# Attention in chunks of 64 tokens as four 64x64 tiles of TensorE, heads exchanged in odd chunks

## The chip, the cores and the metric

One core of a Trainium2 chip runs the whole kernel. The metric is device microseconds of one execution, from the host's launch to the end on the core. Times are medians of several runs; the profile is one execution taken by the hardware profiler.

## The reference

Linear attention with a decay per head, over 4 sequences of 768 tokens, 8 heads of 64, and behind it a SwiGLU layer on the 3072 rows of 512:

```python
block = 64
for b in range(nb):
    intra = einsum('bhic,bhjc->bhij', qb, kb) * Dmask          # lam ** (i - j), i >= j
    intra = einsum('bhij,bhjd->bhid', intra, vb)
    inter = einsum('bhid,bhde->bhie', qb * lam_pow, kv_state)  # lam ** (i + 1)
    out[:, :, sl] = intra + inter
    kv_state = lam_block * kv_state + einsum('bhsd,bhse->bhde', kb * rev_pow, vb)
x = out as rows of (token, head * 64)
xn = x / sqrt(mean(x * x) + 1e-6) * rms_g
g = xn @ w_gate; val = xn @ w_val                              # 512 x 1536
y = (g * sigmoid(g) * val) @ w_out                             # 1536 x 512
```

All is float32. The result of the attention does not depend on the size of the chunks, so a kernel may choose its own.

## The kernel before

Tokens go in six groups of 512 (`G`, four chunks of 128, `GC`), heads in four pairs (`NP`). Two heads of 64 fill the 128 partitions. So there are 24 pairs of work, `Pair(m, p)`, group m and pair of heads p. The attention works in float32, and each float32 matmul of the program is two instructions on TensorE.

A pair has four kinds of matmul, each for four chunks and two heads. `scores` multiplies keys and queries of a chunk, 64 rows by 128 columns of the array for each head, into two banks of PSUM (`pa`, banks ps0 and ps1). `state_sums` sums keys and values over the 128 tokens of a chunk, 128 rows by 64 columns (`pst`). `mix_chunks` multiplies the decayed scores with the values, 128 rows by 64 columns (`po`), and `mix_states` adds the state before the chunk times the query, 64 rows by 64 columns, into the same `po`. VectorE multiplies the scores with the decay table (`decay_a`, one operation of 128x512 for each head) and carries the state from chunk to chunk (`states`, one operation of 128x64 for each chunk). ScalarE scales the keys (`decay_k`), copies the output into the rows (`keep_output`) and squares it (`keep_squares`); GpSimd scales the queries (`decay_q`). `powers` makes the decay tables by scans on VectorE.

The layer behind runs in units (group m, 128 hidden columns f). Units of groups 0 and 1 use plain products (`gate`, `val`, L761) with weights split into f16 halves, and beside them the weights are converted, scaled and summed on VectorE, ScalarE and GpSimd. From group 2 on (after some 260 us of the span) each unit is a two-by-two scheme of seven smaller products (L948, 128x256). The output products are L780 to L782. Units of that scheme take turns between the banks ps0, ps1 and the banks pg, pv; a pair of the next group is laid beside them: its scores in a unit that leaves ps0 and ps1 free, the rest in the next one, which leaves pg and pv free. `pst` and `po` lie in pg and pv (po0 and po1 for a few early pairs). The small column sums for the weights (L445, L321) use ps1.

The order of all engines comes from a planner in the kernel's own code (`Plan`): each step has an engine, a cost, a due time, what it reads and writes and which buffers it opens. `SHIFTS` moves the due times of single steps by their number. The planner charges TensorE a small price where the kind of matmul changes (`TURN`).

## Time and profile before

| | |
|---|---|
| median of 3 runs | 653.84 us (653.78 to 654.0) |
| span of the profiled execution | 652.3 us; of its whole time the page gives no more |
| TensorE busy (matmuls) | 642.5 us, 98%, 5016 matmuls |
| VectorE busy | 433.9 us, 67%, 836 instructions |
| ScalarE busy | 334.8 us, 51%, 676 instructions |
| GpSimd busy | 149.4 us, 23%, 133 instructions |

A matmul's time runs from its start to its modelled end, and several are in flight at once, so the busy time of one group of matmuls is more than the time it takes up: a row of "x16" has the time from the first start to the last end. How far apart matmuls start has to be read from the starts. "Idle before" is the time in which an engine had nothing, and behind the arrow stands what ended it.

### The profile page before, as it was taken

The page shows a single profiled execution, that of the slowest core. Times are in us where ns is not written, and L with a number is a line of the kernel's source. Part 1 is how long each engine was busy: PE and PEld are TensorE (multiplying, and loading weights), DVE is VectorE, ACT ScalarE, POOL GpSimd, SP SyncE. Part 2 cuts the span into 40 slices and gives each one's busy share as a digit, 9 for nine tenths or more (in the row PEclk, how much of TensorE's full clock was granted, in tenths as well). Part 3 has the DMA queues.
Part 4 walks back from the last instruction along what each step waited for, and adds up shares of the span by engine and source line. Part 5 has one row for each costly group of instructions (what it writes and reads, how often), then busy time and mean ns, then how long its engine had stood idle before and what let it go on. Part 6 is the DMA issues. An engine that isn't in the chain of part 4 may idle for free.

```text
span 652.3 us, 12342 instructions
## 1 busy us (share of the span) xinstructions
PE 642.5 (98%) x5016; PEld 442.0 (68%) x5016; DVE 433.9 (67%) x836; ACT 334.8 (51%) x676; POOL 149.4 (23%) x133
## 2 busy tenths in 40 slices
PE   7999999999999999999999999999999999999997
PEld 6846564755656645777777777777777777777774
DVE  6798897968997659656589634587543488544334
ACT  2876876756774444444545533335444334533332
POOL 2213040003477654354703011002010101100000
PEclk9999999999999999999999999999999999999999
DMA  8956653411002400101300311100220000000001
GB/s 328 327 211 221 238 191 133 169 58 65 1 24 91 146 2 1 65 4 63 130 2 2 130 65 65 66 1 1 97 99 1 2 2 1 33 33 1 2 1 65
DMA packets 14314, 51.13 MB, mean 78 GB/s; under 512 B 1713, under 2 KB 1969, under 8 KB 12849
## 3 DMA queue, kind: packets, MB, share of 16 engines
q1 hardware_dynamic: 13968, 50.21, 21.5%
q8 instruction: 39, 0.64, 0.4%
q10 hardware_dynamic: 288, 0.14, 0.1%
q14 instruction: 19, 0.15, 0.1%
HBM read 44.05 MB, written 6.29 MB: 77 GB/s over the span
## 4 chain that ended last, share of the span: by engine, by line
PE 95%; DVE 3%; DMA 1%; issue 0%; POOL 0%; ACT 0%; DVEq 0%; ACTq 0%
PE pa L948 20%; PE pb L948 15%; PE acc L780 10%; PE acc L782 10%; PE acc L781 10%; PE pg L761 9%; PE pv L761 9%; PE pa L507 4%; PE po L572 3%; PE po L583 3%; PE pst L540 2%; PE pss L628 1%; DMA cs<-in_consts_dram 1%; DVE xn L714 0%; DVE pw L159 0%
## 5 line engine op out<-in xcount | busy, mean ns | idle before, releaser
L996 ACT COPY tx<-pa 128x256 f32<-128x256 f32 x144 | 53.6, 372 | 136.6 <-PE pa L948 134.9
L782 PE MATMUL acc<-wo,hh 128*128 128x512 f16 (+1 forms) x288 | 110.2, 383 | 0.0
L781 PE MATMUL acc<-wo,hh 128*128 128x512 f16 (+1 forms) x288 | 110.1, 382 | 0.0
L1000 DVE TENSOR_TENSOR tx<-pb,tx 128x256 f32<-128x256 f32 x96 | 40.8, 425 | 65.3 <-PE pb L948 59.9
L780 PE MATMUL acc<-wo,hh 128*128 128x512 f16 x216 | 81.8, 379 | 0.0
L1004 DVE TENSOR_TENSOR sg<-pb,tx 128x256 f32<-128x256 f32 x48 | 20.4, 425 | 78.5 <-ACT tx L996 76.1
L948 PEld LDWEIGHTS <-wo 128*128 128x128 f16 x576 | 54.9, 98 | 23.2 <-issue 1.7
L761 PE MATMUL pg<-x,wg 128*128 128x512 f16 x288 | 67.7, 379 | 1.3 <-DVE wg L467 0.7
L761 PE MATMUL pv<-x,wv 128*128 128x512 f16 x288 | 67.5, 379 | 0.0
L948 PEld LDWEIGHTS <-wg 128*128 128x128 f16 x576 | 56.3, 98 | 16.2 <-issue 0.3
L1041 ACT CAST hh<-sg 128x512 f16<-128x512 f32 (+2 forms) x73 | 44.7, 612 | 35.6 <-DVE sg L1016 15.4
L948 PEld LDWEIGHTS <-wv 128*128 128x128 f16 x576 | 56.3, 98 | 8.3 <-issue 0.2
L531 POOL TENSOR_TENSOR qkv<-qkv,pw 128x512 f32<-128x512 f32 x24 | 32.2, 1342 | 77.3 <-PE pa L507 71.1
L761 PEld LDWEIGHTS <-wg 128*128 128x128 f16 x288 | 26.8, 98 | 33.8 <-issue 2.4
L761 PEld LDWEIGHTS <-wv 128*128 128x128 f16 x288 | 27.1, 98 | 32.9 <-issue 1.2
L1052 DVE TENSOR_TENSOR hh<-sg,hh 128x512 f16<-128x512 f32 x53 | 39.2, 739 | 7.8 <-ACT hh L1041 3.5
L1016 DVE SCALAR_TENSOR_TENSOR sg<-tx,cv,sg 128x512 f32<-128x512 f32 (+1 forms) x49 | 39.3, 803 | 5.6 <-ACT sg L1008 0.7
L948 PE MATMUL pa<-tx,wo 128*128 128x256 f16 x288 | 39.4, 273 | 0.0
L948 PE MATMUL pb<-tx,wo 128*128 128x256 f16 x288 | 39.3, 273 | 0.0
L948 PE MATMUL pa<-x,wv 128*128 128x256 f16 x288 | 39.3, 273 | 0.0
L948 PE MATMUL pa<-x,wg 128*128 128x256 f16 x288 | 39.3, 273 | 0.0
L948 PE MATMUL pb<-x,wv 128*128 128x256 f16 x288 | 39.3, 273 | 0.0
(186 smaller groups left out, 1152.1 us busy)
## 6 DMA issues: line engine op xcount, KB each, us to landing
qkv<-in_qkv_dram SPq DMA_DIRECT2D x48, 512.0 KB, 4.8
raw_gv<-in_weights_dram SPq DMA_DIRECT2D x11, 1024.0 KB, 6.3
raw_o<-in_weights_dram SPq DMA_DIRECT2D x12, 512.0 KB, 4.1
out_dram<-o SPq DMA_DIRECT2D x23, 256.0 KB, 2.1
partial<-in_weights_dram SPq DMA_DIRECT2D x2, 512.0 KB, 11.1
out_dram<-o ACTq DMA_DIRECT2D x1, 128.0 KB, 2.4
out_dram<-o SPq DMA_DIRECT2D x1, 128.0 KB, 2.4
cs<-in_consts_dram ACTq DMA_DIRECT2D x1, 8.0 KB, 4.7
```

Of the source, the lines that this page charges most:

```text
L507: nc.tensor.matmul(self.pa[j][:, c, :], self.kT[r, c, :], self.qT[r, c, :], start=True, stop=True,)
L531: eng.tensor_mul(self.qT, self.qT, pw[:, p : p + 1, :].broadcast_to([P, GC, P]))
L761: nc.tensor.matmul(ps, w[:, kk, :], x[:, kk, :], start=i == kk == 0, stop=i == 2 and kk == NK - 1,)
L780: nc.tensor.matmul(acc[:, cols], hl[:, ts_], oh, start=first, stop=False, skip_group_check=True)
L781: nc.tensor.matmul(acc[:, cols], hh[:, ts_], ol, start=False, stop=False, skip_group_check=True)
L782: nc.tensor.matmul(acc[:, cols], hh[:, ts_], oh, start=False, stop=last, skip_group_check=True)
L948: nc.tensor.matmul(ps, w(ow, k), x(ox, k), start=first and i == k == 0, stop=i == 2 and k == 1, skip_group_check=True,)
L996: nc.scalar.copy(self.kept[:, i], self.pa)
L1000: nc.vector.tensor_add(self.val[:, half], self.pb, self.kept[:, i])
L1016: nc.vector.scalar_tensor_tensor(sg, self.val[:, half], cv[:, self.f : self.f + 1], sg, ALU.mult, ALU.mult)
L1041: nc.scalar.copy(self.hh[:, half], self.sg[:, half])
L1052: nc.vector.tensor_sub(self.hl, self.sg, hh)
```

## The change

Chunks of 64 tokens in place of 128. A chunk c of 128 tokens stays the unit of the loops and of the layout; it is now an even and an odd half (o = 0, 1). In odd halves the host has exchanged the two heads of a pair in q, k (both forms), so that every matmul is 64 rows by 64 columns of the array with 64 columns of data, and the four of a step (two heads, two halves) sit on the four quarters of the array. The state is advanced twice in a chunk: to a middle state (`mid`), after the even half, and from there to the state behind the odd half. The middle state is copied with its two halves of partitions exchanged (`turn`, two copies on VectorE of 64x256), as the odd half's query needs it. Sums and outputs share two banks (`pst`, `po`: one bank for each half). Pairs of groups 1 (but its first) and 2 use ps0 and ps1 for these, the others pg and pv or po0 and po1 as before. In a pair, chunk products now come first and state sums right behind them; the squares read the copied rows rather than PSUM. The decay tables are 64 long. `SHIFTS` is new as a whole: some 450 entries in place of some 200. Inputs, loads and stores have the same bytes, but for a smaller table of constants.

```diff
     def powers(p, part):
-        if part < 2:
-            h = 2 * p + part
-            nc.vector.tensor_tensor_scan(
-                mask[:, h, :], lam_b[:, h : h + 1].broadcast_to([P, P]), ident, 0.0,
-                ALU.mult, ALU.add,
-            )
-        else:
-            nc.vector.tensor_tensor_scan(
-                pw[:, p, :], lam_p[:, p : p + 1].broadcast_to([P, P]), zeros, 1.0,
-                ALU.mult, ALU.add,
-            )
+        for s in range(2):
+            lam = lams[s][:, p : p + 1].broadcast_to([P, D])
+            if part == s:
+                nc.vector.tensor_tensor_scan(
+                    mask[:, p, s, :], lam, diagonal, 0.0, ALU.mult, ALU.add
+                )
+            elif part == 2:
+                nc.vector.tensor_tensor_scan(
+                    pw[:, p, s, :], lam, zeros, 1.0, ALU.mult, ALU.add
+                )
...
 
         def __init__(self, m, p):
             self.m, self.p = m, p
-            self.odd = m == 0 and p % 2 or m == 1 and p == 0
+            if m == 0 and p % 2 or m == 1 and p == 0:
+                self.pool, self.banks = ps_out, ("po0", "po1")
+            elif m in (1, 2):
+                self.pool, self.banks = ps_att, ("ps0", "ps1")
+            else:
+                self.pool, self.banks = ps_gv, ("pg", "pv")
...
             for c in chunks:
-                for j, r in enumerate(heads):
-                    nc.tensor.matmul(
-                        self.pa[j][:, c, :], self.kT[r, c, :], self.qT[r, c, :],
-                        start=True, stop=True,
-                    )
...
+                for o, keys in enumerate(lanes):
+                    for s, r in enumerate(lanes):
                         nc.tensor.matmul(
-                            self.pst[r, c, :], self.k[:, c, r], self.v[:, c, r],
+                            self.pa[s][keys, c, :], self.kT[r, c, lanes[o]], self.qT[r, c, lanes[o]],
                             start=True, stop=True,
                         )
...
+        def decay_a(self, s):
+            p = self.p
+            if s == 0:
+                t = att.tile([P, 4, GC, D], F32, tag="a", name=f"a_{self.m}_{p}", bufs=2)
+                self.a, self.mid, self.turned = t[:, :2], t[:, 2], t[:, 3]
+            decay = mask[:, p, s : s + 1, :].broadcast_to([P, GC, D])
+            nc.vector.tensor_mul(self.a[:, s], self.pa[s], decay)
...
+        def state_sums(self):
+            for c in range(GC):
+                for o in range(self.sums_end(c)):
+                    r = lanes[o]
+                    for h, out in enumerate(lanes):
+                        nc.tensor.matmul(
+                            self.pst[o][out, c, :], self.k[r, c, lanes[h ^ o]], self.v[r, c, lanes[h]],
+                            start=False, stop=True, skip_group_check=True,
+                        )
...
         def states(self, chunks=range(GC)):
             m, p = self.m, self.p
+            power = pw[:, p, 0, D - 1 : D]
             for c in chunks:
                 g = m * GC + c
-                if g % SEQ_CH == SEQ_CH - 1:
-                    continue
-                new = state[:, p, g % SLOTS, :]
+                mid = self.mid[:, c, :]
                 if g % SEQ_CH == 0:
-                    nc.vector.tensor_copy(new, self.pst[:, c, :])
+                    nc.vector.tensor_copy(mid, self.pst[0][:, c, :])
                 else:
                     nc.vector.scalar_tensor_tensor(
-                        new, state[:, p, (g - 1) % SLOTS, :], pw[:, p, P - 1 : P],
-                        self.pst[:, c, :], ALU.mult, ALU.add,
+                        mid, state[:, p, (g - 1) % SLOTS, :], power, self.pst[0][:, c, :],
+                        ALU.mult, ALU.add,
                     )
-
-        def mix(self):
-            self.mix_chunks()
-            self.mix_states()
-
-        def mix_chunks(self, chunks=range(GC)):
+                if self.sums_end(c) == 2:
+                    nc.vector.scalar_tensor_tensor(
+                        state[:, p, g % SLOTS, :], mid, power, self.pst[1][:, c, :],
+                        ALU.mult, ALU.add,
+                    )
+
+        def turn(self, eng=nc.vector):
+            copy = nc.scalar.copy if eng is nc.scalar else eng.tensor_copy
+            for s, r in enumerate(lanes):
+                copy(self.turned[r], self.mid[lanes[1 - s]])
...
+        def mix_chunks(self):
             m, p = self.m, self.p
-            if 0 in chunks:
...
-            for c in chunks:
-                for j, r in enumerate(heads):
-                    nc.tensor.matmul(
-                        po[r, c, :], self.v[:, c, r], self.a[:, j, c, :],
-                        start=c == 0, stop=False, skip_group_check=True,
-                    )
+            self.po, self.pst = [], []
+            for o in range(2):
+                t = self.pool.tile([P, 2, GC, D], F32, tag=self.banks[o], name=f"po_{m}_{p}_{o}")
+                self.po.append(t[:, 0])
+                self.pst.append(t[:, 1])
+            for c in range(GC):
+                for o, r in enumerate(lanes):
+                    for h, out in enumerate(lanes):
+                        nc.tensor.matmul(
+                            self.po[o][out, c, :], self.v[r, c, lanes[h]], self.a[r, h ^ o, c, :],
+                            start=c == 0, stop=False, skip_group_check=True,
+                        )
 
...
         def mix_states(self):
-            m, p, po = self.m, self.p, self.po
+            m, p = self.m, self.p
             for c in range(GC):
                 g = m * GC + c
-                if g % SEQ_CH:
-                    for r in heads:
+                for o in range(2):
+                    if o == 0 and g % SEQ_CH == 0:
+                        continue
+                    for h, out in enumerate(lanes):
+                        r = lanes[h ^ o]
+                        st = self.turned[r, c, :] if o else state[r, p, (g - 1) % SLOTS, :]
                         nc.tensor.matmul(
-                            po[r, c, :], state[r, p, (g - 1) % SLOTS, :], self.qT[r, c, :],
+                            self.po[o][out, c, :], st, self.qT[r, c, lanes[o]],
                             start=False, stop=True, skip_group_check=True,
                         )
...
             x = rows[m][0]
             copy = nc.scalar.copy if eng is nc.scalar else eng.tensor_copy
-            copy(x[:, p, :].rearrange("p (c i) -> p c i", c=GC), self.po)
+            to = x[:, p, :].rearrange("p (c o i) -> p c o i", c=GC, o=2)
+            for o in range(2):
+                copy(to[:, :, o], self.po[o])
...
         def keep_squares(self):
             m, p = self.m, self.p
...
-            nc.scalar.activation(sq, self.po, AF.Square)
+            x = rows[m][0][:, p, :].rearrange("p (c i) -> p c i", c=GC)
+            nc.scalar.activation(sq, x, AF.Square)
...
     def pair_scores(q, at):
         n = f"{q.m}_{q.p}"
-        for i in range(2):
-            step("PE", 0.545, at + 0.02 * i, q.scores, range(2 * i, 2 * i + 2), r=[f"q{n}:q", f"q{n}:K"],
-                 w=[f"pa{n}_0", f"pa{n}_1", "turn:pa"],
-                 new=[] if i else [(f"pa{n}_{j}", f"ps{j}") for j in range(2)])
+        step("PE", 0.48, at, q.scores, r=[f"q{n}:q", f"q{n}:K"], w=[f"pa{n}_0", f"pa{n}_1", "turn:pa"],
+             new=[(f"pa{n}_{j}", f"ps{j}") for j in range(2)])
...
         for j in range(2):
-            step("DVE", 0.65, at - 1, q.decay_a, j, r=[f"pa{n}_{j}", f"mask{2 * q.p + j}"], w=[f"a{n}"], new=[] if j else [(f"a{n}", "a")])
+            step("DVE", 0.4, at - 1, q.decay_a, j, r=[f"pa{n}_{j}", f"mask{2 * q.p + j}"], w=[f"a{n}"], new=[] if j else [(f"a{n}", "a")])
...
     def pair_sums(q, at):
         n = f"{q.m}_{q.p}"
-        step("PE", 0.5, at, q.state_sums, r=[f"q{n}:k", f"q{n}:v"], w=[f"pst{n}", "turn:pst"],
-             new=[(f"pst{n}", "po0" if q.odd else "pg")])
+        step("PE", 0.48, at, q.mix_chunks, r=[f"q{n}:v", f"a{n}"], w=[f"po{n}_0", f"po{n}_1", "turn:po"],
+             new=[(f"po{n}_{o}", q.banks[o]) for o in range(2)]
+             + [(f"x{q.m}", f"xs{SLOT_OF[q.m]}")] * (q.p == 0))
+        step("PE", 0.45, at + 0.01, q.state_sums, r=[f"q{n}:k", f"q{n}:v"], w=[f"po{n}_0", f"po{n}_1", f"pst{n}"])
         for i in range(2):
-            step("DVE", 0.58, at - 1, q.states, range(2 * i, 2 * i + 2), r=[f"pst{n}", f"pw{q.p}"], w=[f"state{q.p}"])
+            step("DVE", 1.13, at - 1, q.states, range(2 * i, 2 * i + 2), r=[f"pst{n}", f"pw{q.p}"],
+                 w=[f"state{q.p}", f"mid{n}"])
+        step("DVE", 0.4, at - 1, q.turn, r=[f"mid{n}"], w=[f"a{n}"])
...
-        for i in range(2):
-            step("PE", 0.515, at + 0.01 * i, q.mix_chunks, range(2 * i, 2 * i + 2), r=[f"q{n}:v", f"a{n}"],
-                 w=[f"po{n}", "turn:po"],
-                 new=[] if i else [(f"po{n}", "po1" if q.odd else "pv")] + [(f"x{m}", f"xs{SLOT_OF[m]}")] * (p == 0))
-        step("PE", 0.8, at + 0.05, q.mix_states, r=[f"q{n}:q", f"state{p}"], w=[f"po{n}"])
-        step("ACT", 0.57, at - 1, q.keep_output, r=[f"po{n}"], w=[f"x{m}:h{p}", f"x{m}:l{p}"])
-        step("ACT", 0.59, at - 1, q.keep_squares, r=[f"po{n}"], w=[f"s{n}", f"rows{m}"],
+        step("PE", 0.45, at, q.mix_states, r=[f"q{n}:q", f"state{p}", f"a{n}"], w=[f"po{n}_0", f"po{n}_1"])
+        step("ACT", 0.72, at - 1, q.keep_output, r=[f"po{n}_0", f"po{n}_1"], w=[f"x{m}:h{p}", f"x{m}:l{p}"])
+        step("ACT", 0.59, at - 1, q.keep_squares, r=[f"x{m}:h{p}"], w=[f"s{n}", f"rows{m}"],
...
-                    pair_scores(q, u + 0.62)
-                    pair_sums(q, u + 0.64)
-                    if pair:
-                        pair_mix(pair, u + 0.63)
-                    pair = q
-                elif n == NP:
-                    pair_mix(pair, u + 0.63)
+                    pair_scores(q, u + 1.1)
+                    pair_sums(q, u + 1.4)
+                    pair_mix(q, u + 1.7)
                 elif n == NP + 1:
...
```

## Rows read from the trace of the kernel before

**Rows 1.** The page's head and its first part: span, then busy time of each engine, share of the span and instructions.

```profile
span 652.3 us, 12342 instructions
PE 642.5 (98%) x5016; PEld 442.0 (68%) x5016; DVE 433.9 (67%) x836; ACT 334.8 (51%) x676; POOL 149.4 (23%) x133
```

**Rows 2.** Busy time of each engine in four stretches (us from the span's start, then its length, busy us and instructions of each engine, granted clock, DMA share, GB/s).

```profile
5.00:35.00 30.00, 27.13 (x359) 22.90 (x360) 25.29 (x64) 18.19 (x36) 8.85 (x7) 1.00 0.95 356
35.00:110.00 75.00, 74.01 (x468) 42.56 (x468) 67.59 (x133) 55.34 (x101) 14.04 (x10) 1.00 0.57 205
110.00:260.00 150.00, 149.82 (x951) 88.73 (x950) 118.39 (x226) 88.33 (x160) 62.51 (x54) 1.00 0.18 61
260.00:520.00 260.00, 259.98 (x2278) 191.83 (x2277) 154.81 (x294) 118.15 (x263) 58.22 (x50) 1.00 0.14 50
```

**Rows 3.** What TensorE waited for on other engines (total us, times, longest): the first and the last of seven rows, which sum to 5.6 us.

```profile
PE pa L507 <- DVE a L527: 1.6, 1, 1.6
...
PE po L572 <- DVE sg L1029: 0.2, 1, 0.2
```

**Rows 4.** TensorE in order of time, a pair of a late group: scores, then state sums, chunk products and state products (start, us from the first start to the last end, what).

```profile
485.76 0.38 PE L782 MATMUL acc<-wo,hh 128*128 128x512 f16 x1
486.07 1.16 PE L507 MATMUL pa<-qkv 64*128 64x128 f32 x16
487.17 0.83 PE L948 MATMUL pa<-tx,wo 128*128 128x256 f16 x6
487.83 0.38 PE L780 MATMUL acc<-wo,hh 128*128 128x512 f16 x1
488.05 0.38 PE L781 MATMUL acc<-wo,hh 128*128 128x512 f16 x1
...
494.14 0.38 PE L782 MATMUL acc<-wo,hh 128*128 128x512 f16 x1
494.45 0.57 PE L540 MATMUL pst<-qkv 128*64 128x64 f32 x12
494.85 1.04 PE L572 MATMUL po<-a,qkv 128*64 128x128 f32 x16
495.82 0.83 PE L948 MATMUL pa<-tx,wo 128*128 128x256 f16 x6
...
497.14 0.82 PE L948 MATMUL pb<-tx,wo 128*128 128x256 f16 x6
497.88 1.09 PE L583 MATMUL po<-qkv,state 64*64 64x128 f32 x16
498.91 0.61 PE L948 MATMUL pa<-tx,third 128*128 128x256 f16 x4
```

**Rows 5.** TensorE in order of time around state sums that stand alone.

```profile
303.93 0.82 PE L948 MATMUL pb<-x,wg 128*128 128x256 f16 x6
304.68 0.69 PE L540 MATMUL pst<-qkv 128*64 128x64 f32 x16
305.30 0.72 PE L948 MATMUL pa<-tx,wo 128*128 128x256 f16 x5
```

**Rows 6.** TensorE in order of time where kinds of attention matmul follow one another.

```profile
19.90 1.09 PE L572 MATMUL po<-a,qkv 128*64 128x128 f32 x16
20.93 0.87 PE L583 MATMUL po<-qkv,state 64*64 64x128 f32 x12
21.73 1.09 PE L572 MATMUL po<-a,qkv 128*64 128x128 f32 x16
22.66 0.63 PE L540 MATMUL pst<-qkv 128*64 128x64 f32 x16
```

**Rows 7.** The scores' and the state sums' matmuls by line (count, ns of one: least, median and most, first and last start in us, form).

```profile
L507 PE MATMUL pa<-qkv x384: 271/272/535, 5.3 to 505.1; 64*128 64x128 f32 x192
L540 PE MATMUL pst<-qkv x320: 219/222/270, 7.4 to 512.9; 128*64 128x64 f32 x160
```

**Rows 8.** The chunk products alone, L572, in three stretches (length, busy us and count of matmuls and of weight loads, clock, DMA).

```profile
0.00:35.00 35.00, 5.47 (x80) 4.26 (x80) 1.00 0.90 329
35.00:260.00 225.00, 8.75 (x128) 6.82 (x128) 1.00 0.31 109
260.00:520.00 260.00, 11.75 (x176) 9.42 (x176) 1.00 0.14 50
```

**Rows 9.** VectorE by line and form: decay, an operation of 128x256 out of PSUM, state, and the two scans of the decay tables.

```profile
L1000 DVE TENSOR_TENSOR tx<-pb,tx 128x256 f32<-128x256 f32 x96 | 40.8, 425 | 65.3 <-PE pb L948 59.9
L527 DVE TENSOR_TENSOR a<-pa,mask 128x512 f32<-128x512 f32 x48 | 31.1, 683 | 9.2 <-PE pa L507 6.8 <-PE po L572 2.3
L555 DVE SCALAR_TENSOR_TENSOR state<-state,pw,pst 128x64 f32<-128x64 f32 x64 | 17.8, 279 | 2.9 <-PE pst L540 1.2
L154 DVE TENSOR_TENSOR_SCAN mask<-cs,ident 128x128 f32<-128x128 f32 x8 | 3.7, 498 | 0.0
L159 DVE TENSOR_TENSOR_SCAN pw<-cs,wg 128x128 f32<-128x128 f32 x4 | 2.5, 655 | 0.0
```

**Rows 10.** ScalarE by line and form: a copy of 256 columns out of PSUM, and the copy of a pair's output.

```profile
L996 ACT COPY tx<-pa 128x256 f32<-128x256 f32 x144 | 53.6, 372 | 136.6 <-PE pa L948 134.9 <-DVE tx L1000 0.7 <-DVE sg L1004 0.5
L595 ACT COPY x<-po 128x512 f32<-128x512 f32 x24 | 14.1, 586 | 29.3 <-PE po L583 29.2
```

**Rows 11.** VectorE in order of time, where it makes the first group's normalised rows.

```profile
31.73 2.71 DVE L714 SCALAR_TENSOR_TENSOR xn<-x,gs,pr 128x512 f32<-128x512 f32 x4
```

88 lines of the change are left out of this document (37 added, 51 removed), and 83 rows, old and new, of the table SHIFTS.

## The prediction

> **What bounds the kernel now.** I read the page's busy line first, then the busy times by stage, then what TensorE waited for. TensorE is busy for 642.5 of 652.3 us [rows 1], and in each stage after 35 us it is busy almost without a gap at the full granted clock of 1.00 [rows 2]. All its waits on other engines, seven kinds, sum to 5.6 us, none of them over 1.6 us [rows 3]. So from about 35 us to the end the time is the sum of TensorE's pitches. VectorE comes second, and by stage the picture differs: 25.3 of 30 us before 35 us, 67.6 of 75 us up to 110 us, 118.4 of 150 us up to 260 us, and only 154.8 of 260 us where the attention of the last groups runs beside the two-by-two products [rows 2]. The change takes time from the first engine and gives time to the second, so each stage has to be asked apart.
>
> **What one pair costs TensorE before.** A late pair stands in three pieces [rows 4]. An f16 matmul of 512 columns has a pitch of 0.216 us (487.83 to 488.05), six of 256 columns take 0.655 us. The piece is counted from where the ordinary product before it would have ended to where the next begins. Scores: 485.76 + 0.216 = 485.98 to 487.17, 1.19 us. State sums and chunk products: 494.14 + 0.216 = 494.36 to 495.82, 1.46 us. State products: 497.14 + 0.655 = 497.80 to 498.91, 1.11 us. Together 3.77 us.
>
> **What it costs after.** Each old matmul of 128 columns becomes 64x64 pieces of 64 columns, issued by fours that sit on the four quarters of the array. No row of before shows four quarters at work at once. The nearest row is the state sums: two column halves, 64 columns each. Sixteen of them last 0.63 us with a single one at 0.22 us, so seven steps of two take 0.41 us, 0.059 us a step [rows 6, 7]. Halves by rows overlap as well: sixteen scores of 0.27 us each fit into 1.16 us [rows 4, 7], and so do the diagonal quarters of the state products. I take 0.059 us for a step of four. The lower end is a gain that the streaming of 64 columns excludes (0.059 us already is the pace of 64 columns); the upper end is two steps, 0.117 us, if only two quarters run together.
>
> Scores are 8 such steps, chunk products 8, state sums 8 (7 in a sequence's last chunk), state products 8 (7 in its first). Changing the array's shape costs too. An isolated block of 8 steps, the state sums at 304.68, takes from 303.93 + 0.655 = 304.585 to 305.30, 0.715 us, of which the 8 steps are 0.47 us: 0.245 us for changing in and out [rows 5]. Between blocks of one shape nothing is lost: state sums follow chunk products of the same shape 0.93 us after these began (21.73 to 22.66), where state products of another shape follow after 1.03 us (19.90 to 20.93) [rows 6]. After the change all four kinds have one shape, and chunk products and state sums are planned next to each other. So a pair is three blocks: 0.715 + (0.715 + 0.47) + 0.715 = 2.61 us. That saves 3.77 - 2.61 = 1.16 us a pair on TensorE, 28 us for 24 pairs. By the chunk products' counts (16 a pair) the pairs lie as 5 before 35 us, 8 up to 260 us, 11 after [rows 8].
>
> **What VectorE pays.** Rows by form give the prices [rows 9]. Removed in a pair: two decays of 128x512 at 0.683 us. Added in their place: two of 128x256, for which the row of the same shape out of PSUM has 0.425 us; 0.52 us less. Every chunk now has a middle state, so 80 more updates of 128x64 at 0.279 us and 16 copies, now one per sequence start as before: 96 more in 24 pairs with the copies unchanged, 1.1 us a pair more. The exchange of halves is two copies of 64x256, which no row shows. They lie between the copy-sized update (0.279 us) and the 128x256 operation (0.425 us) or a little under; I take 0.3 us, so 0.6 us a pair (0.4 to 0.85). Sum: +1.2 us a pair (1.0 to 1.45). The decay tables shrink: 8 scans of 128 at 0.498 and 4 at 0.655 us, 6.6 us, become 16 scans of 64; at half length each some 4.6 us, so -2.0 us (-2.6 to +1.4, if a scan's cost hardly falls with its length).
>
> ScalarE copies an output in two parts of 256 columns (0.372 us each) instead of one of 512 (0.586 us) [rows 10], +0.16 us a pair; it is busy 118 of 260 us in the late stage and 55 of 75 us in the tightest, and I cost this at nothing. If its cover were gone it would be 3.8 us. The squares now read the copy in SBUF and wait for it; that hangs on the same engine's order and costs nothing. GpSimd's work on q is the same; loads and stores are the same bytes.
>
> **Stage by stage.** Before 35 us: 5 pairs add 6.0 us and the scans take off 2.0, so VectorE goes from 25.3 to 29.3 of 30 us. TensorE's 5.8 us can't come out there; the chain through the states is longer too. The normalised rows that open the first product leave VectorE from 31.73 us on [rows 11], behind all of that. I take +1 us (-3 to +4). From 35 to 110 us: 3 pairs bring VectorE from 67.6 to 71.2 us, while TensorE would need 75 - 3.5 = 71.5 us. Both would be full, so I count nothing. From 110 to 260 us: 5 pairs, VectorE 124.4 of 144.2 us; of TensorE's 5.8 us I count 4.7 us. So 4.7 us for 35 to 260 us (0 to 9.3). After 260 us: 11 pairs, 12.8 us, with VectorE at 168 of 247 us; I count 12.0 us (8 to 12.8), as states, exchange and state products are now a chain within one unit. The new shifts move steps on every queue, the loads on SP's too. What they could give back alone is what TensorE waits for now, 5.6 us; what they could lose has no row. I take 0, with 4 us to either side.
>
> Sum: 12.0 + 4.7 - 1.0 = 15.7 us. The profiled execution's span is 652.3 us, 1.5 us under the median of 653.84 us, which I take as what lies around the span: 636.6 + 1.5 = 638.1 us.
>
> **Rivals.** (1) TensorE's saving comes out in full: the stage before 35 us unchanged, 9.3 and 12.8 us after it, and some 5 of the 5.6 us of waits closed as well: 653.8 - 27, about 627 us. For it speaks that the work of the weights on VectorE need not be done where it stands, against it that 35 to 110 us has no room on VectorE. 0.10.
>
> (2) The four quarters don't run together, as the fastest sustained pitch of any row is 0.029 us from matmul to matmul [rows 6], and four at that pitch are 0.117 us. A pair then takes 30.7 steps x 0.117 + 3 x 0.245 = 4.33 us against 3.77, so 0.56 us more; with 24 pairs and VectorE's additions before 110 us (about 3 us) this gives 653.8 + 13 + 3, about 670 us. It decides from (3.77 - 0.735) / 30.7 = 0.099 us a step. Against it speaks that halves by rows, by columns and on the diagonal overlap. 0.08.
>
> The Trainium skill, "TensorE: Matmul & The Clock Gate", section "Wait — 56ns, not 53.3ns?", says that matmuls never start closer than about 25 ns, however small. As an estimate from that page a step of four would be 0.100 us, a pair 3.8 us, and the gain would be gone. By that rule rival (2) holds; the rows here show no sustained pitch under 0.029 us and can't refute it.
>
> (3) The early stage turns on VectorE and a bank. In groups 1 and 2 the outputs now lie in the two banks of the scores, from the chunk products to the copy (some 0.94 + 2.2 + 0.6 + 0.5 + 0.75 us and the waits between), and the small sums for the weights need one of the same banks. If each of those 7 pairs holds up the weights, and so the first products, by 2 us beyond the saving, the 12 us after 260 us are gone: 655 us, slower. It decides from 1.7 us a pair. For it speaks VectorE's 90% from 35 to 110 us. 0.04.
>
> (4) After 260 us the chain (1.2 us of products, 8 updates of 0.279 us, 0.6 us of copies, 0.5 us of products, 0.75 us of copying out) holds banks that the next unit needs. That is some 5.4 us, where it is 4.5 us now from the state sums to the end of the state products (494.45 to 498.91) and 0.6 us for the copy [rows 4, 10]. A wait of 2 us a pair would turn 638 into 660 us. 0.02. (5) Gains and losses cancel within 0.2%, which is about what a measurement of this kernel can tell from no change (652.5 to 655.1 us): 0.04.
>
> **How the numbers follow.** The forecast has 0.72. Its own bounds are 653.8 - 3 - 9.3 - 12.8 = 628.7 and 653.8 + 4 - 0 - 8 = 649.8 us; with 4 us for the shifts, 624.7 to 653.8. The range of 624 to 655 us takes in these, rivals (1) and (5) and the edge of (3), and leaves out some 0.12. Faster: 0.72 + 0.10 = 0.82; the same 0.04; slower 0.14.
>
> **What would show it.** Steps of four with a pitch near 0.06 us and a block of scores near 0.7 us confirm the term of TensorE; pieces near 1.1 us show rival (2). Windows after 260 us should be 12 us shorter in sum. If the first product starts later than before and VectorE is busy over 95% from 5 to 110 us, the early terms are right. I am wrong on the early stage if it gets shorter by more than 5 us, and wrong on the late one if TensorE shows waits on VectorE or ScalarE there.

## The result and the profile after

The changed kernel takes 658.1 us (median of 20 runs, 655.42 to 663.04), the kernel before 654.31 us beside it; the ratio is 1.0056 with a 95% interval of 1.0039 to 1.0074. It is slower by 0.6%, where 638.1 us was forecast, and its time lies outside the range of 624 to 655 us.

First the page of the changed kernel, its span and busy times, which answer to [rows 1].

```profile
span 658.5 us, 15668 instructions
PE 630.7 (96%) x6572; PEld 426.2 (65%) x6572; DVE 466.8 (71%) x984; ACT 330.6 (50%) x700; POOL 151.6 (23%) x134
```

TensorE has 11.8 us less work and yet the span is 6.2 us longer. That is more than the 3.8 us between the medians: the profiled execution of the changed kernel took 660.3 us, 2.2 us more than its median. The stretches of [rows 2], now:

```profile
5.00:35.00 30.00, 25.26 (x644) 22.47 (x645) 23.63 (x80) 12.13 (x28) 6.33 (x5) 0.89 0.80 291
35.00:110.00 75.00, 68.54 (x671) 39.18 (x671) 63.63 (x144) 52.98 (x104) 13.61 (x11) 1.00 0.52 184
110.00:260.00 150.00, 146.66 (x1135) 81.11 (x1134) 128.55 (x253) 92.26 (x170) 58.56 (x50) 1.00 0.22 78
260.00:520.00 260.00, 252.53 (x3093) 183.51 (x3092) 178.89 (x377) 118.41 (x276) 67.17 (x55) 1.00 0.17 54
```

TensorE's gaps are in every stretch, the largest share before 110 us; VectorE is not fuller there than before (63.6 of 75 us), and the granted clock of the first stretch is 0.89. What TensorE waited for, beside [rows 3]:

```profile
PE pa L965 <- ACT tx L1013: 5.1, 3, 2.6
PE pn L447 <- ACT junk L442: 3.9, 5, 1.5
PE po L546 <- issue: 2.6, 1, 2.6
PE pb L965 <- DVE tx L1017: 1.6, 2, 0.9
```

The largest wait is for ScalarE's copies of the products' banks, the second for squares of weights on ScalarE, the third for nothing that a semaphore shows.

**The work itself became as cheap as forecast.** TensorE in order of time, a late pair (and the scores of the one behind it), to be held against [rows 4]:

```profile
485.10 0.38 PE L799 MATMUL acc<-wo,hh 128*128 128x512 f16 x1
485.41 0.70 PE L516 MATMUL pa<-qkv 64*64 64x64 f32 x32
485.92 0.65 PE L585 MATMUL po<-a,qkv 64*64 64x64 f32 x32
486.39 0.64 PE L546 MATMUL po<-qkv 64*64 64x64 f32 x28
486.96 0.39 PE L797 MATMUL acc<-wo,hh 128*128 128x512 f16 x1
```

Eight steps of four quarters take 0.47 us from the chunk products' start (485.92) to the sums' (486.39), 0.059 us a step. The three blocks take 486.96 - 485.10 - 0.216 = 1.64 us; the state products, read in the same way at 491.2 us, 0.73 us. That is 2.37 us where 3.77 us was read before and 2.61 us forecast; the 16 pairs in the table below come to 2.65 us each.

For the whole span I laid the trace's single matmuls out by their starts: a product has its own pitch (0.216 us for 512 columns, 0.109 for 256), and what lies beyond it up to the next start counts to attention if an attention matmul stands there, else as a wait. Products come to 531.2 us in all kernels here. What moves:

| us | before | after | later decays | all orders |
|---|---|---|---|---|
| start of the first product | 33.6 | 41.7 | 41.8 | 36.9 |
| last start of the first 216 products | 96.1 | 104.8 | 104.2 | 99.3 |
| waits in the next 216 products | 0.8 | 5.5 | 5.6 | 5.6 |
| attention from there on, 16 pairs | 59.6 | 42.4 | 42.6 | 42.6 |
| waits behind the 864th product | 0 | 9.5 | 4.0 | 3.8 |

(The last two columns are experiments.) So 17.2 us were saved, and 8.7 + 4.7 + 9.5 us lost: +5.7 of the 6.2 us; the rest is scattered.

**Where the 8.7 us before 105 us begin.** TensorE in order of time, in the sums of pair (0,3), and the stretches around it:

```profile
22.14 0.52 PE L546 MATMUL po<-qkv 64*64 64x64 f32 x20
25.31 0.69 PE L546 MATMUL po<-qkv 64*64 64x64 f32 x12 [2.65 <-issue]
...
41.74 1.31 PE L778 MATMUL pg<-x,wg 128*128 128x512 f16 x4 [0.48 <-ACT wg L465]
```

```profile
20.00:25.00 5.00, 2.66 (x102) 2.33 (x93) 2.67 (x10) 2.32 (x4) 1.10 (x1) 0.95 0.87 303
25.00:30.00 5.00, 4.40 (x60) 3.68 (x63) 3.71 (x13) 1.13 (x3) 0.00 (x0) 0.50 0.24 93
```

TensorE stops between two matmuls of one block with no semaphore to wait for, while the DMA share is 0.87; VectorE and ScalarE idle behind it. In the trace's DMA records a 16 KB packet of the instruction queue runs from 22.83 to 23.72 us. TensorE has 1556 more matmuls than before (5016 to 6572), each with a weight load, and that queue 51 packets for 39 (its row in the changed kernel, then before):

```profile
q8 instruction: 51, 0.84, 0.5%
```

```profile
q8 instruction: 39, 0.64, 0.4%
```

The granted clock is 0.50, 1.2 GHz, in the whole stretch from 25 to 30 us. In the kernel before no such stop is in the trace.

That the stop is the fetch of TensorE's own instructions can be counted. 13144 matmuls and weight loads over 51 packets are 258 for each, about 256. In the 18 traces here TensorE stops 32 times for over 0.2 us with nothing that a semaphore shows. In 30 of these the count of matmuls and weight loads started so far is 193 or 194 above a multiple of 256, always the same place in a packet's worth, and TensorE starts again 1.3 to 1.6 us after a packet has ended. The packet before this stop was late and not slow: its 0.89 us are less than the median of 1.00 us, but 399 matmuls and weight loads lie between the start of the packet before it and its own. Most versions of the changed kernel have two such stops, one at 13 to 15 us (0.2 to 1.7 us) and this one.

**Where the 9.5 us after 260 us begin.** ScalarE, TensorE and SyncE's queue around 480 us, in order of time:

```profile
478.81 0.37 ACT L1013 COPY tx<-pa 128x256 f32<-128x256 f32 x1 [1.00 <-PE pa L965]
482.54 0.51 ACT L523 ACTIVATE qkv<-qkv,mask 128x256 f32<-128x256 f32 x1 [3.36 <-DMA qkv<-in_qkv_dram]
482.95 0.35 ACT L1013 COPY tx<-pa 128x256 f32<-128x256 f32 x1
```

```profile
480.35 0.38 PE L799 MATMUL acc<-wo,hh 128*128 128x512 f16 x1
483.36 0.38 PE L965 MATMUL pa<-x,wg 128*128 128x256 f16 x2 [2.63 <-ACT tx L1013]
```

```profile
475.12 2.28 SPq L87 DMA_DIRECT2D qkv<-in_qkv_dram  x2
477.45 1.39 SPq L857 DMA_DIRECT2D out_dram<-o  x3
```

ScalarE, in order, stands at a decay of k (L523) whose load (the second of the two) was issued at 475.5 us and shares the DMA engines with three stores; the copy that frees TensorE's bank (L1013) is behind it. The load lands 7 us after its issue; the planner counts 4.6. In the kernel before no load of q, k and v that was issued after 260 us took over 5.1 us. From 260 to 520 us ScalarE waits so for 10.0 us in 5 places, before for 1.1 us in one (the changed kernel, then before):

```profile
ACT qkv L523 <- DMA qkv<-in_qkv_dram: 10.0, 5, 3.4
```

```profile
ACT qkv L517 <- DMA qkv<-in_qkv_dram: 1.1, 1, 1.1
```

### The profile page after: what moved, and what is told of

It reads as the page before. It is cut to its first block, busy times and chain, and to the rows that moved or that the text cites. A ratio compares the mean times of both kernels' runs of the same rounds, so it can differ in the third digit from the quotient of the medians.

```text
span 658.5 us, 15668 instructions
## 1 busy us (share of the span) xinstructions
PE 630.7 (96%) x6572; PEld 426.2 (65%) x6572; DVE 466.8 (71%) x984; ACT 330.6 (50%) x700; POOL 151.6 (23%) x134
## 4 chain that ended last, share of the span: by engine, by line
PE 67%; DVE 7%; DMA 3%; ACT 2%; issue 1%; POOL 0%; SPq 0%; DVEq 0%; ACTq 0%
PE pa L965 17%; PE pb L965 13%; PE acc L797 8%; PE acc L799 7%; PE acc L798 7%; PE pv L778 5%; PE pg L778 4%; DMA qkv<-in_qkv_dram 3%; PE po L585 1%; PE po L600 1%; PE pa L516 1%; PE po L546 1%; DVE a L560 1%; DVE a L573 1%; DVE state L565 1%
## 5 line engine op out<-in xcount | busy, mean ns | idle before, releaser
L1013 ACT COPY tx<-pa 128x256 f32<-128x256 f32 x144 | 53.1, 369 | 113.0 <-PE pa L965 80.6
L965 PEld LDWEIGHTS <-wv 128*128 128x128 f16 x576 | 56.3, 98 | 12.8 <-issue 0.9
L1069 DVE TENSOR_TENSOR hh<-sg,hh 128x512 f16<-128x512 f32 x53 | 44.0, 830 | 11.8 <-ACT hh L1058 11.3
L1025 ACT ACTIVATE sg<-sg,cg 128x256 f32<-128x256 f32 x48 | 24.4, 509 | 35.4 <-DVE sg L1021 35.2
```

The costliest lines, as they stand in the source:

```text
L965: nc.tensor.matmul(ps, w(ow, k), x(ox, k), start=first and i == k == 0, stop=i == 2 and k == 1, skip_group_check=True,)
L1013: nc.scalar.copy(self.kept[:, i], self.pa)
L1025: nc.scalar.activation(self.sg[:, half], self.sg[:, half] if t else self.pa, AF.Silu, scale=cg[:, self.f, 0:1],)
L1069: nc.vector.tensor_sub(self.hl, self.sg, hh)
```

## Experiments

Theory: TensorE's saving is real; it is given back by (a) a later start, from VectorE's longer chain and a stalled instruction fetch, (b) ScalarE's orders behind late loads, (c) weights that come late. Rivals: VectorE's added work costs it in all stages, through banks that are held; or the new list of shifts does. Kernels differ from the changed one, or the one named, only by what is shown or said; `move(i, j)` takes step i of the finished order to the place before step j.

**1. Decays of k later.**

```diff
         order = plan.run()
+        starts = {i: t for t, i in order}
+        sums = {fn.__self__: starts[i] for i, (_, _, _, fn, *_) in enumerate(plan.steps) if fn.__name__ == "state_sums"}
+        for i, (eng, _, _, fn, *_) in enumerate(plan.steps):
+            if fn.__name__ == "decay_k" and fn.__self__.m >= 3:
+                t = max(starts[i], min(starts[i] + 6.0, sums[fn.__self__] - 2.5))
+                order.remove((starts[i], i))
+                order.insert(next(k for k, (s, _) in enumerate(order) if s > t), (starts[i], i))
```

> The changed kernel, with the two decays of k on ScalarE of every pair from group 3 on placed up to 6 us of the planner's time later in ScalarE's order, behind copies of the products' banks; all else is as in the changed kernel (658.1 us). My theory: after 260 us TensorE waits because ScalarE stands in order at a decay of k whose load has not landed (2.7 us at 280 us, 3.4 us at 482 us), so that the copies that free the products' banks come late. Then those two idle stretches of ScalarE go, TensorE's waits of 1.98 us at 279 us and 2.63 us at 480 us go with them, and the time falls by 4 to 6 us, to 652 to 654 us. Rival: the late stages wait for VectorE's longer chain of states or for the two banks which it holds. Then moving the decays changes nothing, 657 to 659 us, and the waits at 279 and 480 us stay.

654.27 us, 3.8 us less than the changed kernel's median; ratio to before 0.9988 (0.9971 to 1.0005). What TensorE still waits for from 260 to 520 us:

```profile
PE pb L965 <- DVE tx L1017: 1.6, 2, 0.9
PE pa L965 <- ACT tx L1013: 0.8, 2, 0.5
```

Both long waits are gone, and nothing of VectorE's or the banks' took their place (the 1.6 us behind VectorE stood there before). The theory holds; the 3.8 us fall just short of its 4 to 6 us. Of the 4.0 us of waits that the table still has in the late part, these rows name 2.4.

**2. Conversions first.**

```diff
+        for i in (110, 221, 222):
+            move(i, 123)
```

> The changed kernel, with three steps of VectorE in the first 35 us placed earlier in its order: the turn of pair (0,2) and the two conversions of the first block of weights now stand ahead of the states of pair (0,3). My theory: the first product is 8.1 us later than before (41.7 against 33.6 us) because VectorE, in order, comes to these conversions at 29.6 us, after it idled 2.7 us behind TensorE's stall. Then the conversions run at 23 to 26 us, the first product starts 2 to 4 us earlier (38 to 40 us) and the time falls by 2 to 4 us to 654 to 656 us. Rival: the first product waits for the normalisation, which hangs on the last pair's attention; then it starts within 0.7 us of 41.7 us, and the time stays at 657 to 659 us.

659.18 us; the first product at 41.2 us. The conversions did run earlier (from 23.7 us, not 29.6), and it brought 0.5 us, although the stop was shorter in this trace, 0.94 us. Here the rival held: the first product hangs on the normalisation and so on the last pair's attention, whose states the moved conversions now hold up by 1.9 us.

**3. First weight loads later.** In `load_gv`, and the two steps behind the states of pair (0,3):

```diff
+            if f == 1:
+                nc.vector.memset(t[:, 0, :1, 0].bitcast(F32), 0.0)
...
+        for i in (12, 13):
+            move(i, 110)
```

> The changed kernel, with the first load of raw gate and value weights (and the raw output weights that follow it in the queue) made to wait for a tiny write of VectorE that stands behind the states of pair (0,3), so that it is issued at about 24 us or later and not at 19.4 us. My theory: TensorE's stall of 2.65 us in the middle of the sums of pair (0,3), which no semaphore explains, is the fetch of its own instructions, held up by this load (the instruction queue's packet took 0.89 us there). Then the stall goes or shrinks under 1 us, TensorE's granted clock stays at full from 25 to 30 us, and the first product starts 2 to 5 us earlier (37 to 40 us): 653 to 656 us. Rival: the fetch is too slow for this many small instructions in any case; then a stall of 2 us or more stays at about the same matmul, and the time is 657 to 660 us. If later waits for the weights take the gain back, the first product is early and the time is not.

659.25 us, first product at 40.4 us. TensorE's stops, and the stretches (DMA share is the last column but one):

```profile
28.46 0.44 PE L587 MATMUL po<-a,qkv 64*64 64x64 f32 x11
30.94 0.57 PE L587 MATMUL po<-a,qkv 64*64 64x64 f32 x21 [2.03 <-issue]
```

```profile
20.00:25.00 5.00, 3.73 (x102) 3.18 (x95) 4.17 (x17) 1.91 (x4) 0.71 (x1) 1.00 0.09 35
25.00:30.00 5.00, 3.74 (x109) 3.12 (x108) 4.55 (x11) 4.22 (x10) 1.59 (x1) 1.00 0.96 347
...
35.00:40.00 5.00, 4.95 (x45) 4.29 (x45) 4.84 (x13) 2.65 (x6) 1.15 (x1) 0.56 0.50 156
```

The stop is gone from 22 us, where the DMA engines now idle, and stands at 28.9 us, where the loads now are, 256 matmuls and weight loads further on; the clock falls behind it instead. So it follows the loads. The gain failed with it.

**4. No first weights' load at all from 21 to 30 us.** As 3, but:

```diff
-            move(i, 110)
+            move(i, 153)
```

> The changed kernel, with the first load of raw gate and value weights (and the loads behind it in the queue) made to wait for a tiny write of VectorE behind the mean of the first normalisation, so that no load is under way from about 21 to 30 us; all else as in the changed kernel. My theory: without loads beside it the fetch of TensorE's instructions is quick, no stall over 0.5 us is left between 20 and 32 us, and the granted clock stays at full there; VectorE's longer chain remains: first product at 38 to 40 us, against 41.7 us. The time is no shorter, since the second block of weights comes 5 us or more too late, 660 to 668 us. Rival: the stall is not from the loads; then it stays and the first product is at 41 us or later.

663.8 us, first product at 44.2 us: late, because ScalarE then waited 5.6 us for the load of those weights, and VectorE behind it for 5.8 us, ahead of the normalisation. But the stop shrank to this, and the clock stays at 1.00 from 20 to 35 us:

```profile
22.77 0.45 PE L548 MATMUL po<-qkv 64*64 64x64 f32 x12 [0.22 <-issue]
```

This is one execution, and run 9 below has a stop of 0.36 us with the loads in their place, so the shrinking alone does not prove that the loads made it; that no stop at all was left at 22 us in run 3 says more.

**5. The kernel before with more small matmuls.** Behind the sums of each pair of group 0:

```diff
+            if m == 0:
+                ps = ps_out.tile([P, DM], F32, tag="po3", name="unread3")
+                for n in range(88):
+                    i = o = heads[n % 2]
+                    nc.tensor.matmul(ps[o, :D], ident[i, o], ident[i, o], start=True, stop=True)
```

> The kernel before with 88 more small matmuls (64x64 quarters of the unit matrix, into a bank that nobody reads) behind the sums of each of the four pairs of group 0, as many as the change adds to each pair; all else as before. They cost TensorE time of their own, at most 2.6 us per pair if two run side by side. My theory: TensorE's stall of 2.65 us in the changed kernel comes from the fetch of its instructions, which are used up faster than they are fetched while the loads fill the DMA engines. Then the kernel before, too, shows one or more stalls of over 0.8 us ended by no semaphore between 12 and 35 us, where it had none. Rival: the stall belongs to the new tiles or to the order of the changed kernel; then no such stall appears, and the first product is later only by the matmuls' own time, 5 to 10 us.

678.2 us (one run). The count in that text is wrong: 88 matmuls are 176 instructions a pair, and the change adds 65. So they took 5.1 us a pair, at 0.058 us for two. One stop came where before had none:

```profile
12.20 0.74 PE L549 MATMUL unread<-ident 64*64 64x64 f32 x19
14.58 0.38 PE L549 MATMUL unread<-ident 64*64 64x64 f32 x5 [1.63 <-issue]
```

It stands where the count is 194 above a multiple of 256, the place at which the versions of the changed kernel stop at 13 to 15 us, and ends 1.5 us after a packet. So the stop needs neither the new tiles nor the new order.

**6. No exchange.** 

```diff
-            for s, r in enumerate(lanes):
-                copy(self.turned[r], self.mid[lanes[1 - s]])
+            self.turned = self.mid
```

> The changed kernel without the exchange of the middle state's halves: the two copies of VectorE for each pair (28 pairs, 0.6 us each, 17 us of VectorE in all) are left out and TensorE reads the middle state where it stands, so the part of the output that comes from middle states is another one. My theory: VectorE's added work costs time only in the first 35 us, where the chain from sums to states to exchange to the last products stands on the path; the time falls by 1 to 3 us, to 655 to 657 us, and TensorE's waits after 260 us stay. Rival: VectorE's added work is what gives the saving back in all stages, through the banks that are held until it is done; then half of its added work gone takes 6 to 10 us off, 648 to 652 us, most of it after 260 us.

652.7 us, 5.4 us less; ratio to before 0.9959 (0.9931 to 0.9988), with executions from 646 to 655 us (24 pairs, 15.8 us of VectorE). No stop at the sums of pair (0,3), first product at 37.4 us; after 260 us TensorE's waits for ScalarE's copies stay, 4.9 us. Of the 5.2 us between the two traces 3.5 lie before the end of the first 216 products. The place is mostly the theory's, the size between the two.

**7. States as short as before.** One update a chunk, no exchange.

```diff
-                mid = self.mid[:, c, :]
+                last = self.pst[self.sums_end(GC - 1) - 1][:, GC - 1, :]
+                new = state[:, p, g % SLOTS, :]
...
-            for c in range(GC):
+            for c in reversed(range(GC)):
...
-                        st = self.turned[r, c, :] if o else state[r, p, (g - 1) % SLOTS, :]
+                        st = state[r, p, (g - (o == 0 or self.sums_end(c) == 1)) % SLOTS, :]
```

> The changed kernel with VectorE's work on states as short as before: one update for each 128 tokens instead of two, no exchange; the products with states read other states than they should and go through the chunks backwards, so that part of the output is another one. Loads and TensorE's instructions are as in the changed kernel. My theory: VectorE's chain is most of the later first product: 35 to 37 us against 41.7 us (37.4 us when only the exchange was left out), and the time falls by 6 to 9 us to 649 to 652 us, all of it before 160 us; the waits at 279 and 480 us stay. Rival: the number of TensorE's instructions and their fetch set the start; then the first product stays at 38 us or later and the time is no lower than without the exchange, 653 us or more.

652.84 us, ratio to before 0.9967 (0.9945 to 0.9989); stop 0.38 us, first product at 36.1 us. So 5.6 of the 8.1 us at the start go with this edit. They are not the chain's alone, as the stop shrank by 2.3 us with it. The time misses the 649 to 652 us and hardly differs from run 6, and the long waits after 260 us stay (4.4 us). Of the 9.7 us between the two traces 5.9 lie before the 432nd product, 1.7 between it and the 864th, and some 2 behind: VectorE's work costs most at the start, little later.

**8 to 10. The exchange elsewhere** (on top of 1): all of group 0's on ScalarE; one of its two copies on ScalarE for groups 0 and 1; both on GpSimd for groups 0 and 1. The second is

```diff
-            copy = nc.scalar.copy if eng is nc.scalar else eng.tensor_copy
             for s, r in enumerate(lanes):
+                copy = nc.scalar.copy if self.m < 2 and s else eng.tensor_copy
                 copy(self.turned[r], self.mid[lanes[1 - s]])
```

> The kernel with the later decays of k (the first experiment, 654.3 us), and with the exchange of halves of the four pairs of group 0 on ScalarE instead of VectorE; ScalarE stands idle from 22.3 to 28.8 us of the changed kernel. My theory: in the first 35 us VectorE's chain of states and exchange stands on the path. Leaving the exchange out brought the first product from 41.7 to 37.4 us. On another engine it still takes its 0.6 us in the chain, but no longer holds VectorE's states and conversions behind it: half of that comes back, first product at 39 to 40.5 us, 651.5 to 653 us. Rival: only the length of the chain counts; then the first product stays at 41.5 us or later and the time at 654 to 655 us.

> As the kernel with the later decays of k (654.3 us), with one of the two copies of the exchange on ScalarE and the other on VectorE, side by side, for the pairs of groups 0 and 1. My theory: the exchange takes 0.35 us and not 0.6 us in the chain of each early pair, and VectorE is freed of half of it: first product at 39.5 to 41 us, 652 to 653.5 us. Rival (ScalarE's copies come later than VectorE's would have, because ScalarE works in order): first product later than 41.7 us, 654 to 657 us.

> As the kernel with the later decays of k (654.3 us), with the exchange of the pairs of groups 0 and 1 on GpSimd. My theory: GpSimd's copies are slower than VectorE's (its elementwise work on 128x512 takes 1.27 us against about 0.7 us), so the chain of each early pair grows by about 0.6 us, while VectorE is freed: the two about cancel, first product at 40.5 to 42.5 us, 653 to 656 us. Rival: VectorE's occupancy is all that counts; then it is as good as leaving the exchange out: first product near 37.5 us, 649 to 651 us.

651.55, 651.12 (ratio 0.9932, 0.9907 to 0.9957) and 651.61 us, with first products at 38.8, 37.6 and 38.8 us. All three gain some 3 us; for GpSimd I had expected none. That a slower engine does as well suggests that freeing VectorE counts more than the length of one exchange. The stops differ too, 0.9, 0.4 and 1.9 us, so the first products do not price the exchange alone.

**11, 12. Loads of output weights behind others** (on top of the divided exchange): in SyncE's order each load of raw output weights goes behind the next one or two loads; then only those of blocks 2 to 4. Both begin alike (`n, i` run over the loads in their order, `place` has the steps' places):

```diff
+            if fn.__name__ == "load_o" and 2 <= args[0] < NF:
+                ahead = [j for j in loads[n + 1 : n + 4] if plan.steps[j][3].__name__ != "load_o"][:2]
+                ahead = [j for j in ahead if place[j] < place[lifts[args[0]]] - 3]
```

> The kernel with the later decays and the divided exchange (651.1 us), with each load of raw output weights from the third block on placed behind the next one or two loads of SyncE's queue. My theory: between 40 and 140 us TensorE's small waits (5 us from 99 to 151 us, 4.5 us before that, against 0.8 and 2.5 us in the kernel before) come from weights that are loaded late, because SyncE stands in order at a load of output weights whose buffer VectorE frees late (13 us at 38.9 to 52.8 us of the changed kernel), with loads of other weights and of q, k and v behind it. Then those loads are issued earlier, the waits before 160 us fall by 2 to 4 us, and the time to 647 to 649.5 us. Rival: the loads behind it have no free buffer either, or VectorE, 97% busy from 35 to 45 us, sets the pace of the conversions; then the time stays at 650 to 652 us.

> The kernel with the later decays and the divided exchange (651.1 us), with the loads of output weights of blocks 2, 3 and 4 alone placed behind the next one or two loads. Moving all of them took TensorE's waits for norms of weights from 1.5 to 0.3 us (36 to 157 us), but a later one of them then came too late, and TensorE stood 2.3 us at 107 us. My theory (SyncE's order makes the small waits): with three moved, the old waits stay away and the new one goes; waits up to 151 us fall from 9.5 us to 6 or 7 us, and the time to 648 to 650 us. Rival (VectorE's pace makes them): they only change places, 8.5 us or more of them stay, and the time is 650 to 652 us.

649.04 and 649.42 us (ratio 0.9919, 0.9902 to 0.9936, for the second). The waits for norms of weights go, but others come: waits up to the 432nd product are 9.2 and 8.8 us, 9.5 without. By the waits the rival holds, by the median the theory, within the scatter of runs. Undecided.

The early programs of 9 and 12 are the same up to 38 us, and so are those of the changed kernel and 1. The length of the stop differs by execution, and that prices it. Run 9, then run 12:

```profile
23.03 0.45 PE L546 MATMUL po<-qkv 64*64 64x64 f32 x12 [0.36 <-issue]
...
37.64 0.88 PE L778 MATMUL pg<-x,wg 128*128 128x512 f16 x2 [0.49 <-ACT wg L465]
```

```profile
24.61 0.45 PE L546 MATMUL po<-qkv 64*64 64x64 f32 x12 [2.00 <-issue]
...
40.19 0.39 PE L778 MATMUL pg<-x,wg 128*128 128x512 f16 x1 [0.49 <-ACT wg L465]
...
25.00:30.00 5.00, 4.55 (x97) 3.83 (x96) 4.12 (x13) 2.13 (x6) 0.49 (x1) 0.70 0.64 197
```

A stop longer by 1.64 us makes the first product later by 2.55 us; the granted clock of 0.70 behind it, where run 9 has 1.00, is probably part of that. Runs 13 and 14, alike too up to their first product, have stops of 0.63 and 1.18 us, both at a clock of 1.00, and their first products are 0.43 us apart.

**13, 14. The first scale earlier**, alone on run 9 and with run 12:

```diff
+        for i, before in ((231, 133), (232, 134), (137, 143)):
+            move(i, before)
```

> The kernel with the later decays and the divided exchange (651.1 us), with three steps placed earlier: the scale of the first block of weights ahead of the four scalings of the normalised input on VectorE (2.7 us), and on ScalarE its first half-precision copy and one of the input's. My theory: the first product at 37.6 us waits for this copy, which waits for the scale behind the four scalings; it starts 0.5 to 2 us earlier, and the time falls by 0.5 to 1 us. Rival: the input's own copies end the wait, or the products stall after the first; then the time does not change by over 0.4 us.

> The run before with the three steps placed earlier that brought the first product from 37.6 to 36.4 us in the profile (scale and first copy of the first weights, a copy of the input). If both edits add, 647.5 to 649.5 us; if the products only wait later for what comes behind, as the earlier run without a gain in the median says, no better than the run before, within 0.5 us.

651.38 us and 648.86 us. The first product comes at 36.4 and 36.9 us, 1.2 and 3.3 us earlier than in runs 9 and 12 (the latter with a stop of 1.2 us, not 2.0), and the median does not move by more than 0.6 us: the time is lost again behind it. The last is the best version here: ratio to before 0.9915 (0.9901 to 0.9929), 0.85% faster.

**15, 16. Both kernels with an empty list of shifts.**

```diff
+    SHIFTS = {}
```

> The changed kernel with its list of priority shifts emptied: the order of all engines is what the planner makes of the costs and due times. With the next run it tells the tiling from the list. My theory: the losses come from the new chains (states, exchange, loads, fetch), not from the list, which was only fitted to them; without the list the changed kernel loses 5 to 20 us, to 663 to 678 us, and it stays within 6 us of the kernel before without its list. Rival: the new list is what loses the time; then it is faster without the list than with it, under 656 us.

> The kernel before with its list of priority shifts emptied. My theory: it loses 5 to 15 us, to 659 to 669 us, about as much as the changed kernel does without its list. Rival: the list of before is worth much more than that of after (over 10 us more), so that the list, and not the tiles, decides the sign.

670.77 and 663.25 us. Without lists the new tiles lose 7.5 us, a little more than I had set as a limit; with them 3.8 us. So the new list is no cause of the loss: it takes back 12.7 us, the old one 9.3 us (against the 653.9 us beside it).

## Why the prediction was wrong

TensorE's saving came as forecast. What failed is the price of what takes it back. By the starts of the products in the two traces, the first product comes 8.1 us later, where 1 was forecast; from there to the 864th (some 260 us) it takes 2.3 us less, where 4.7 was forecast; and from the 864th to the last 0.3 us more, where 12.0 less was forecast.

- **TensorE's term** (a step of four at 0.059 us, 2.61 us a pair) was right, and rival 2 with it wrong. Matmuls start 0.0147 us apart on average inside a block of 32. The Trainium skill, "TensorE: Matmul & The Clock Gate", section "Wait — 56ns, not 53.3ns?", has a floor of about 25 ns from start to start; the trace shows less, four quarters together, and the measurement decides. The trace of the kernel before had the answer already: in its scores and sums single starts stand 0.007 us apart, two by two. The forecast of 4.7 + 12.0 us behind 110 us stands beside 17.2 us measured.
- **VectorE's term** was right: updates and copies (22.5 + 22.4 + 3.5) against 17.8 us and the old copies, the exchange 15.8 us (0.66 us a pair for 0.6), decays 18.5 against 31.1 us, scans 4.7 us for a forecast 4.6.
- **"I take +1 us (-3 to +4)" for the stage before 35 us** failed: +8.1 us at the first product. I priced VectorE's occupancy there and not the chain (sums, eight updates, exchange, last products, pair after pair), and not the number of TensorE's instructions. Runs 6 to 10 shorten the chain and gain, and the count at the stops, run 3 and the pair 9 and 12 show the stop. How the 8.1 us divide isn't settled, since the stop is shorter in runs 6 to 10 as well. By the price of the two pairs (2.55 / 1.64 and 0.43 / 0.55) a stop of 2.65 us is 2 to 4 us, an estimate.
- **"Both would be full, so I count nothing" for 35 to 110 us** came out near its number (the first 216 products take 0.5 us longer from first to last start) by luck: VectorE is less full than before, 63.6 us and not 71.2. What had no term is waiting behind that: the next 216 products, from 105 to 157 us, wait 4.7 us more, which takes back much of the 7 us that attention saves from there to 260 us. They wait for weights, most of all for ScalarE's squares of them (3.7 us from 36 to 157 us); whether SyncE's order or the conversions' place makes them late is open (11, 12).
- **"12.0 us (8 to 12.8)" after 260 us** was right as work and wrong as time. The step that failed is "loads and stores are the same bytes", costed at nothing with the shifts' "0, with 4 us to either side". The bytes are the same, but the loads now land up to 7.3 us after their issue, k's decay stands on ScalarE before its load has landed, and ScalarE's copies free the banks of TensorE. TensorE's waits there are 9.5 us, and moving the decays alone brought 3.8 us (run 1); what makes the 4.0 us of waits that are left is open. The prediction named this sign, TensorE waiting for ScalarE there, but gave it no price.
- **Rivals 3 and 4** (banks held by the pair) hardly came: the waits named were for copies of the products' own banks, TensorE waited once, 0.6 us, for the copy of a pair's output (L614), and run 1 left no such wait. **The squares behind the copy** show no price: in run 1 TensorE waits for none of them after 260 us.

The Trainium skill, "Runtime: NRT & Kernel Launch", section "Instruction fetch mechanics", says that an engine's instructions come in blocks of 16 KB by a DMA queue of their own while it works, mostly hidden. The packets agree; that they stay hidden does not here.

## What to carry to other kernels

When a matmul is cut into quarters, count the instructions as well as the time: a stretch of many small ones beside heavy loads can stop TensorE for its own fetch, and the granted clock can fall behind it (0.50 here, but 1.00 behind the 1.9 us of run 10). When an engine that works in order frees the bound engine's banks, look at each of its steps that reads a load, and set it where the load has surely landed. A saving on the bound engine is only as good as the next chain: list for each stage what would be late once the bound engine is not.

## What I had not expected of the hardware

TensorE restarts 1.6 us after its 16 KB packet has ended (23.72 to 25.31 us; 1.3 to 1.6 us in all traces), so a late packet costs more than its own 0.89 us. A step costs the same whether two quarters share it or four: two diagonal quarters that write one bank take 0.058 us (run 5: 176 instructions in 5.1 us, 0.029 us each), four quarters into two banks 0.059 us (0.0147 us each). And the length of such a stop is no property of the program: 0.36 and 2.00 us in two executions of the same instructions. That may be why the changed kernel scatters more (655.4 to 663.0 us, 653.8 to 657.5 us before); no run here shows it.
